# Attention and a Hyena gate on one core: gate tiles evicted by pairs of banks, spectra evicted by pairs, three table fetches, and a new order

## The chip, the cores and the metric

The kernel runs on one core of one Trainium2 chip. The metric is the device time of one execution in microseconds (us), lower is better, as the median of several executions. All matrix products are done in float16 or bfloat16 with float32 sums in PSUM; inputs and output are float32.

## The reference

Four batches of eight attention heads over 768 positions with 64 values each; every query sees the 96 positions up to its own and the first 8, with a distance bias whose slope depends on the head. The result, as 768 x 512 for each batch, goes through a Hyena gate: one projection into three parts, a circular convolution of the middle part along the sequence, a product of all three, and an output projection.

```
# q, k, v: (4, 8, 768, 64)
scores = q @ k^T / 8 - slope[h] * dist           # kept: own 96 positions, first 8
a = softmax(scores);  x = (a @ v) as (4, 768, 512)

proj = x @ w_proj                                # (512, 1536)
x1, x2, x3 = proj[..., :512], proj[..., 512:1024], proj[..., 1024:]
X2 = rfft(x2, axis=1);  H = rfft(filter_fft, axis=0)
y = x1 * irfft(X2 * H) * x3
out = y @ w_out                                  # (4, 768, 512)
```

## The kernel before

The kernel builds a graph of steps first and emits it afterwards. Each step (`Plan.op`) names the engines that may run it, what it reads and writes, and which PSUM banks it fills (`acq`) or empties (`use`). There are eight banks of 2 KB for each partition; they are cut from four tiles of two banks (`self.wide`), so banks 0 and 1, 2 and 3, 4 and 5, 6 and 7 are neighbours, and `Bank.two()` is a view over both of such a pair.

The order is written out by hand in the string `ORDER`. Each word is the number of a step, the letter of its engine (P TensorE, A ScalarE, V VectorE, G GpSimd, S SyncE) and the banks that it fills: `223P0` is step 223 on TensorE into bank 0. `schedule()` reads the words and `emit()` writes the instructions in that order. An engine runs its own instructions strictly in the order of the string and waits, by semaphores, for what the next one needs. A word such as `i1b4` is a matmul on zeros into bank 4 whose result nobody reads ("busy matmul", `busy`, L313). The string has 13 of them. DMA transfers are issued by the same queues: loads of inputs from GpSimd (POOL in the profile, L333), a few loads, the transposing transfers of batch 3 and all stores from SyncE (SP).

The work on one batch, in the names that the profile shows:

- **Loads.** q, k and v come as float32 and land as float16 in `qn`, `kn`, `vn`. In batch 0, q and k come in blocks of two heads (`load_pair`). Three of the four blocks go through GpSimd, the fourth through SyncE into `ot` as float32, and is cast.
- **Transposes.** TensorE turns q and k into `QT` and `KT` (L743 the pairs of batch 0, L786 the others). ScalarE or VectorE copies them out of their bank (L317, the helper `copy`). Batch 3 uses transposing DMA transfers instead.
- **Scores and exponentials.** For each pair of heads and each of three groups of key blocks, `scores` fills two neighbouring banks (L812). ScalarE takes the exponential of both in one instruction of 864 columns into `E` (L824), twelve for each batch. In batch 0, TensorE adds the distance bias in the bank beforehand (L598 to L605); in the others VectorE multiplies by a mask (L836).
- **Values.** `values` multiplies `E` by `vn`, with a column of ones for the sum (L862 and L867). VectorE takes the reciprocal, and VectorE or ScalarE scales the result into `xn` (L886, L891). TensorE transposes it (L914) into `xT`.
- **Gate.** For each of the four column blocks j of x1 and x3 and each half s of the sequence, `gate` computes two tiles of 128 x 384 (360 or 408 in batch 3): four matmuls each (L977, or L979 and L982 in batch 3), every tile into a bank of its own. The x1 tile is scaled into one of four staging buffers `x1` (helper `times`, L321 on ScalarE). The x3 tile is copied into `gt` by ScalarE (L991), and VectorE multiplies the two in place; or VectorE multiplies straight from the bank. There are 32 such pairs of tiles.
- **Convolution.** `butterfly` and `folded` fold `xT` on VectorE. The middle projection is done on the folded rows (L1050) and evicted to `ab`. `spectra` transforms it in three pairs of slots (L706): one matmul of 512 columns into a bank for each slot, each bank evicted to `X` by an instruction of its own (L317). VectorE multiplies by the filter's spectrum (`h1`, `h2`). The spectrum of the filter itself is computed once, early (`spectrum`, L715 on TensorE, its sums on VectorE). `inverses` turns back into `eo` (L1137 to L1142), `mixed` and `gated` combine the halves and multiply by `gt` into `y` (L1192 to L1197).
- **Output.** Six output tiles for each batch (L1101), evicted to `ot` (L321) and stored by SyncE. The last one is done in two halves of 256 columns.

The order interleaves these: while batch b is convolved, the attention of batch b + 1 runs between. Ahead of it all stand setup steps: the tables of sines for the transforms (`tables`: angles by TensorE, reduced by ScalarE and VectorE, L462 the copy on ScalarE, L476 the sine), the distance masks on GpSimd, and one small activation on ScalarE, a sine on two values, ahead of anything else there.

The lines that set how a pair of spectra is evicted (`PAIR_X` is empty in this kernel, so the second form is used for all twelve pairs):

```python
if (b, n) in self.PAIR_X:
    bks = [g.bank(), g.bank()]
    self.transform(b, pair, bks)
    g.op("AV", self.evac(1024), lambda e: self.copy(
        e, X[:, pair[0]:pair[0] + 2], bks[0].two()), use=bks, ...)
for s in () if (b, n) in self.PAIR_X else pair:
    bk = g.bank()
    self.transform(b, (s,), [bk])
    g.op("AV", self.evac(512), lambda e, s=s, bk=bk: self.copy(e, X[:, s], bk.f32()), ...)
```

Of the kernel before, what the change touches and what calls it, by code (L numbers as in the profile page):

```python
# [41 lines left out]
0V 32G 19S 4V 5V 34V 28S i1b0 i1b1 16S 8G 33V i1b2 15V 209A i1b3 3G 210A 54V 9V 206A i1b4 13V 204A 59A i1b5 22G 208A  # L42
1V 56V 6V 207A i1b6 57V 205A 25G 11V i1b7 21A 10V i1b0 24G 211A 223P0 53V 216V 35G 84P23 23G i1b1 51V 20V i1b4 2A 27G
213V 224A i1b5 18A 233P1 55V 58V 225V 218P4 26G 17V 234A 64P5 235V 219A 50G 52V 104P6 226V 65A 220V 38G 105V 76P0
106P5 77A 42G 221V 29V 78P6 222A 39G 107V 66A 227A 79A 41G 62P0 60V 239V 228P5 63A 80V 36G 212V 43G 85P 30V 90P4 37V
236V i1b7 215V 44G 81P01 61V 108V 91V 87P67 86A 40G 88P 240V 14V 92P4 229A 89A 73P23 31S 93V 82P 74P 67P67 75A 214V
12V 68P 83A 241V 70P23 230V 217V 231V 71P 69A 112P01 113P 72A 246V 109P45 272G 110P 94A 114A 115P23 247V 273G 101P67
111A 95P01 248V 274G 96P 102P 249V 116P 97A 98P45 280G 250V 99P 117A 118P01 282G 251V 103A 123P23 100A 119V 270G 124V
158P67 252V 125V 253P4 271G 120V 133P23 255P5 281G 159V 134V 160V 258P0 256A 260P1 279G 254A 135V 163P67 261A 257V 46G
259A 266P23 164V 128P45 165V 47G 268A 136P0 267A 372P1 48G 129V 130V 370P6 373A 166P7 285G 121P2 167V 131P3 263P45  # L50
371A 7V 132V 287G 368P1 137V 265A 126P3 374V 369V 161P0 122A 288G 397P5 127A 162V 382P67 264A 398V 377P23 45G 380P01
383A 395P4 189V 286G 399V 144P5 378A 396V 169P6 49G 195V 146A 188V 381A 402P23 499G 375P45 196V 174P7 403A 197V 275G
153P0 190V 176A 198V 148P1 171A 191V 496G 376A 155V 440P6 154P7 199V 284G 441A 150V 405P45 192V 156A 407P23 289G
400P01 200V 406A 193V 183P6 157V 379V 408A 290G 139P7 442P4 401A 194V 444P5 201V 500G 138P2 443V 445A 143P3 141A 384V
446A 185A 449P45 454P01 140A 145V 293P6 450A 278G 262V 404V 455A 452P23 283G 276S 447P45 149P7 409V 453A 277S 497G
242P0 202V 151A 305P1 448A 498G 203V 173P7 306A 147V 514G 152V 297P4 142V 456V 291G 295P1 237A 298A 512G 309P5 269V
175A 451V 294A 511G 390P23 243A 319P4 597P6 310A 391V 506G 392V 307P7 320A 598V 244A 507G 296A 317P4 410P23 308V 232A
393P1 599A 508G 318A 411V 299P6 177V 179P7 412V 394A 415P45 245A 321V 513G 300A 669P0 385P23 416V 181A 417V 593P1 505G
670A 595P7 386V 322V 594A 462P45 724G 387V 313P6 596A 301P0 463V 311P1 509G 457P23 302A 464V 314A 388P0 517G 238V 312A
607P45 458V 303V 184P6 723G 459V 413P1 178P7 292G 389V 608A 622P2 304V 168P0 501G 186A 315V 180A 418P3 620P6 623V 504G  # L60
414A 667P7 170A 726S 621V 419A 605P45 515G 602P01 187V 727S 606A 665P6 182V 420P3 624V 733G 172V 603A 668V 460P2 426P4
666V 510G 461A 422V 630P67 428A 632P01 609V 735G 625P23 631A 465P5 421P4 466V 722G 626A 671V 425P6 487V 633A 627P23
721G 488V 478P5 502S 427A 628A 473P0 503S 316V 737G 431P1 480A 490V 423A 738G 489V 600P23 475A 674P67 672P45 433A 634V
430P0 601A 739G 435P1 491V 673A 734G 325P2 424V 329P3 437A 629V 335P4 675A 736G 331P1 530P5 326V 332A 516G 492V 432A
333P2 676V 330A 725G 679P01 334A 677P67 337P3 336A 604V 323P2 680A 732G 518P4 493V 324A 640P01 338A 434V 494V 531A
327P2 731G 483P3 678A 641V 495V 468P5 743G 328A 642V 519A 610P67 339V 740G 635P01 485A 470A 611V 544P4 340V 534P3 612A
728G 636V 341V 520P5 637V 742G 681V 826S 615P01 535A 741G 682P67 521A 616V 342V 545A 467P3 744G 823S 683V 617A 343V
522P2 429V 344V 822S 477P4 523A 345V 472P5 684V 825S 613P2 474A 436P0 469A 348V 538P5 438A 526P6 524P3 614A 643P7 729S
439V 542P0 479A 638P1 346V 532P2 525A 824S 539A 349V 618P3 482P4 533A 850S 543A 476V 362P5 347V 484A 619A 536P0 546V
848S 685P4 537A 687P23 639V 363A 541V 359P1 686A 481V 527A 688V 486V 353P0 689V 644A 891S 360A 834P67 540V 832P45 354A  # L70
827P23 690P1 847S 528V 835A 650P0 691V 828A 529V 829P67 364S 660P1 713V 833A 849S 655P2 652A 547V 661P3 662A 712V 894S
830A 350P0 663A 715V 365P1 657A 892S 664V 351A 714V 851P23 366A 858P67 853P45 471V 893S 859A 552P0 716V 356P1 831V
553A 854A 550P6 730S 558P0 717V 548P7 357A 836V 355S 554P4 852A 367S 656P5 718V 361S 549A 560P1 842P23 658A 719V 556P7
551A 562P5 843V 561A 855V 645P6 559A 557A 646P1 720V 563A 555A 651P7 844V 648A 659V 647A 900P45 845S 856P01 564V 901A
837P23 565V 698P6 857A 838V 352S 707P4 566V 839V 653A 693P5 700A 649V 841S 709A 567V 902P23 897P67 695A 895P01 654V
898A 697P4 568V 846S 860V 702P5 896A 861P67 903A 569V 840S 708P0 862V 570V 692P1 863A 904V 747P2 899V 703P3 694A 710A
910P67 865S 573V 705A 699A 866P01 748A 911V 760P4 701V 864S 704A 867V 912V 868A 762P5 696V 914S 711V 758P6 574V 763A
905P01 571V 761A 870S 766P7 759A 764P4 906V 745P5 767A 572V 869S 765A 749P7 706V 746A 769V 773P6 913S 907V 771P5 774A
751P4 578P2 772A 768V 908S 750A 871P3 775V 752A 753P7 770V 584P6 754A 909S 776V 876P4 585A 755V 779P5 873A 358S 756V
791P7 878A 581P6 792A 757V 780A 783P3 936V 787P7 777P5 788A 887P4 784A 935V 781P7 789P0 872P3 790A 782A 938V 785P1  # L80
575P0 786A 937V 778A 877P1 889A 939V 874A 886P7 793V 940A 587P3 794V 888A 941V 957P4 795A 890V 942V 944P7 958A 796V
588A 590P5 943V 945A 589S 879A 972P3 797V 586S 970P7 591A 959P4 875V 973A 798V 971A 961P5 799V 960A 948P7 974V 962A
800V 579A 963P1 965P5 964A 946P4 580S 802V 966A 592S 882P1 947A 967V 916P5 949A 968V 582A 950P4 952P7 975V 951A 931P2
583S 969V 953A 921P4 884A 955V 576A 997P3 930P1 954V 933A 577S 998A 978P0 880V 982P2 956V 932A 993P3 983A 881P7 803V
994A 980P1 883A 995P2 991P3 801V 996A 976P6 926P7 992A 885V 977A 1000V 925P3 979A 999V 981A 934V 920P6 1001V 927A 985V
928A 915P1 984V 1002V 986A 819P7 929V 917A 1003V 987V 816P3 1004V 820A 988V 918A 1005V 821S 813P2 923A 989V 919V 922A
810P4 990V 817A 1021V 814A 818S 804P5 924V 811A 1019V 815S 1022V 807P2 812S 805A 1020V 1029P3 808A 1006V 1023P5 1008V
# [113 lines left out]

class Fused:
    PERIOD = 40.0
    PAIR_X = ()
    PAIR_AB = ()
    PAIR_EO = ()
    PAIR_T = (1, 2, 3)
# [1175 lines left out]
```

## Time and profile before

| | |
|---|---|
| median of 3 runs | 168.0 us (167.95 to 168.52) |
| the profiled execution, its own time | 167.31 us |
| its span, first to last instruction | 165.6 us |
| granted TensorE clock, mean over the span | 0.977 of full speed |
| moved by DMA | 22.84 MB, mean 138 GB/s |

The profile is one execution. PE is the matmul side of TensorE and PEld its weight loads, which overlap the matmuls; DVE is VectorE, ACT is ScalarE, POOL is GpSimd, SP is SyncE. A line such as L824 is a line of the kernel. "E<-bank" is the output and the input by the program's names. The form behind it (128x864 f16<-128x864 f32) is partitions x elements and type, and x48 the number of instructions. In a timeline the first column is the start in us from the start of the span and the second the length; consecutive instructions of one form are one row, and square brackets give the idle time ahead of it with what ended it. "PE bank" as the waiting side means that TensorE was about to write into a bank; the name behind the arrow is the engine, the tile and the line that released it. The page also cuts the span in 40 slices of 4.1 us; a digit there is a share in tenths. Ends of matmuls are modelled.

### The profile page before, as it was taken

How to read it: one execution, taken by the hardware profiler on the slowest of the kernel's cores; microseconds unless marked ns; L12 is line 12 of the kernel's file. 1: busy time of each engine (PE TensorE's matmuls, PEld its weight loads, DVE VectorE, ACT ScalarE, POOL GpSimd, SP SyncE). 2: the span in 40 equal slices, each digit the busy share in tenths (PEclk: the TensorE clock that was granted, in tenths of full speed). 3: DMA queues.
4: the chain of work that ended last, by engine and by line, in shares of the span. 5: the costliest groups of instructions: out<-in, count | busy, mean ns of one | idle time of the engine just before them, and what ended most of it. 6: DMA issues, size and time to landing. Idle time of an engine off the chain costs nothing.

```text
span 165.6 us, 4471 instructions
## 1 busy us (share of the span) xinstructions
PE 156.5 (95%) x1722; PEld 98.6 (60%) x1722; DVE 151.4 (91%) x351; ACT 149.9 (91%) x308; POOL 73.5 (44%) x94
## 2 busy tenths in 40 slices
PE   6758999999999999999999999999999999999990
PEld 2255756785654787657766655866655754585440
DVE  6698598999998999999999999999999999999940
ACT  3979697799999999999998999999997899999842
POOL 7997489999299996999930000000000000000000
PEclk9985899999999999999999999999999999999999
DMA  5999999999999999999999754603123203430685
GB/s 140 167 173 200 151 161 139 153 170 190 164 156 147 148 143 154 162 164 146 146 110 185 110 127 95 209 16 98 33 60 80 72 0 129 149 110 0 242 314 204
DMA packets 90365, 22.84 MB, mean 138 GB/s; under 512 B 81504, under 2 KB 87016, under 8 KB 90344
## 3 DMA queue, kind: packets, MB, share of 16 engines
q0 software_dynamic: 74880, 12.46, 100.8%
q1 hardware_dynamic: 15464, 10.10, 22.4%
q8 instruction: 13, 0.21, 0.5%
q14 instruction: 8, 0.07, 0.1%
HBM read 25.69 MB, written 6.29 MB: 193 GB/s over the span
## 4 chain that ended last, share of the span: by engine, by line
PE 87%; ACT 7%; DVE 3%; issue 1%; POOL 1%; ACTq 0%; POOLq 0%
PE bank L977 19%; PE bank L1050 13%; PE bank L1101 12%; PE bank L812 7%; PE bank L979 6%; PE bank L862 4%; PE bank L786 4%; PE bank L867 3%; PE bank L706 3%; PE bank L914 3%; ACT E L824 2%; PE bank L598 2%; ACT mask L613 1%; PE bank L604 1%; PE bank L1137 1%; PE bank L1140 1%
## 5 line engine op out<-in xcount | busy, mean ns | idle before, releaser
L824 ACT ACTIVATE E<-bank 128x864 f16<-128x864 f32 x48 | 41.9, 947 | 1.9 <-PE bank L812 1.9
L977 PE MATMUL bank<-xT,w 128*128 128x384 f16 x192 | 36.0, 326 | 0.0
L333 POOL DMA_DIRECT2D vn<-in_v_dram x28 | 25.9, 937 | 3.1 <-DMA w<-in_moe_w_proj_dram 2.9
L977 PEld LDWEIGHTS <-w 128*128 128x128 f16 x192 | 17.3, 98 | 10.7 <-issue 1.1
L1101 PE MATMUL bank<-wo,y 128*128 128x512 f16 (+1 forms) x100 | 22.7, 370 | 0.0
L333 POOL DMA_DIRECT2D kn<-in_k_dram x24 | 21.6, 908 | 0.5 <-issue 0.3
L333 POOL DMA_DIRECT2D qn<-in_q_dram x21 | 18.6, 887 | 6.2 <-PE bank L812 3.4
L836 DVE TENSOR_TENSOR E<-E,mask 128x1728 f16<-128x1728 f16 x18 | 18.6, 1048 | 0.0
L321 ACT ACTIVATE ot<-bank 128x512 f32<-128x512 f32 (+1 forms) x24 | 13.8, 605 | 3.2 <-PE bank L1101 3.1
L991 ACT CAST g<-bank 128x384 f16<-128x384 f32 (+2 forms) x32 | 15.9, 545 | 0.0
L862 PE MATMUL bank<-vn,E 128*128 128x65 f16 x224 | 15.4, 193 | 0.4 <-ACT E L824 0.4
L886 DVE TENSOR_TENSOR xn<-bank,rc 128x512 f16<-128x512 f32 (+1 forms) x20 | 15.6, 789 | 0.2
L1050 PE MATMUL bank<-w,xab 128*128 128x512 f16 x64 | 15.4, 379 | 0.0
L862 PEld LDWEIGHTS <-E 128*128 128x128 f16 x224 | 14.1, 97 | 2.2 <-issue 0.4
L1101 PEld LDWEIGHTS <-y 128*128 128x128 f16 x100 | 9.4, 98 | 9.9 <-DVE y L1197 0.5
L867 PE MATMUL bank<-vn,E 128*128 128x65 f16 x192 | 15.2, 193 | 0.0
L321 ACT ACTIVATE x<-bank 128x384 f16<-128x384 f32 (+2 forms) x28 | 14.4, 537 | 0.5 <-ACT ab L317 0.5
L317 ACT CAST X<-bank 128x512 f16<-128x512 f32 x24 | 13.8, 619 | 0.6 <-PE bank L706 0.5
L317 ACT CAST eo<-bank 128x384 f16<-128x384 f32 x31 | 13.5, 520 | 0.7 <-PE bank L1142 0.7
L867 PEld LDWEIGHTS <-E 128*128 128x128 f16 x192 | 13.2, 97 | 1.5 <-issue 0.6
L317 ACT CAST ab<-bank 128x512 f16<-128x512 f32 x23 | 13.9, 641 | 0.1
L812 PE MATMUL bank<-QT,KT 64*128 64x216 f16 (+2 forms) x224 | 13.6, 244 | 0.2 <-DVE KT L317 0.2
(186 smaller groups left out, 368.4 us busy)
## 6 DMA issues: line engine op xcount, KB each, us to landing
out_dram<-ot SPq DMA_DIRECT2D x23, 256.0 KB, 2.2
vn<-in_v_dram POOLq DMA_DIRECT2D x28, 120.0 KB, 7.7
kn<-in_k_dram POOLq DMA_DIRECT2D x21, 120.0 KB, 6.3
qn<-in_q_dram POOLq DMA_DIRECT2D x18, 128.0 KB, 5.8
w<-in_moe_w_proj_dram POOLq DMA_DIRECT2D x4, 256.0 KB, 6.7
g<-in_moe_filter_fft_dram POOLq DMA_DIRECT2D x1, 768.0 KB, 10.4
kn<-in_k_dram POOLq DMA_DIRECT2D x3, 192.0 KB, 6.4
qn<-in_q_dram POOLq DMA_DIRECT2D x3, 192.0 KB, 6.1
```

Of the source, the lines that this page charges most:

```text
L317: {"A": nc.scalar.copy, "V": nc.vector.tensor_copy, "G": nc.gpsimd.tensor_copy}[e](out, in_)
L321: self.nc.scalar.mul(out, in_, c)
L333: return self.g.op(eng, 0.57 + 0.00035 * nbytes[0] if eng == "G" else 0.5, lambda _: e.dma_start(dst, src), w=w, r=r, nbytes=nbytes, name= ...
L812: nc.tensor.matmul(bs[hh].f32()[:, off:off + w], self.KT[hs, hp, P * m:P * m + P], self.QT[hs, hp, KL * m:KL * m + w], start=(off == 0 and ...
L824: g.op("A", act(864), lambda _: nc.scalar.activation(eo, bs[0].two()[:, :, 0:432].rearrange("p h (m w) -> p h m w", m=2), Act.Exp, scale=s ...
L836: g.op("V", dve(1728, 2), lambda _: nc.vector.tensor_mul(ep, ep, mk), r=[("mask", h) for h in range(hs.start, hs.stop)] + ([("mask0", hp - ...
L862: nc.tensor.matmul(o[:, n, hh], ef[:, at:at + P], vt[:, t, 2 * hp + hh, 0:D + 1], start=first, stop=(t == 0), skip_group_check=True)
L867: nc.tensor.matmul(o[:, n, hh], ef[:, at:at + P], vt[:, t - 1, 2 * hp + hh, 0:D + 1], start=False, stop=True, skip_group_check=True)
L977: nc.tensor.matmul(bk.f32()[:, 0:h], w, self.xT[:, c, lo:lo + h], **kw)
L991: first = g.op("AV", {"A": act(h), "V": 0.0005}, lambda e: nc.scalar.copy(x3, pts[1].f32()[:, 0:h]) if e == "A" else None, use=[pts[1]], w ...
L1050: nc.tensor.matmul(bk.f32(), src[:, c], w[:, c, DM:2 * DM], start=(c == 0), stop=(c == 3))
L1101: nc.tensor.matmul(bk.f32()[:, 0:n], y[:, c, P * t:P * t + P], self.wo[:, c, ns], start=(c == 0), stop=(c == 3))
```

## The change

The change has four parts.

**Gate.** One step now does the eight matmuls of both tiles, the x1 tile into the first and the x3 tile into the second of two neighbouring banks (the loop over the four matmuls of a tile is now the function `gated_tile`). One instruction of 2 x 384 columns, on ScalarE or VectorE, scales both banks into a buffer `x13`, each by the root of the factor that x1 alone was scaled by. There are two such buffers (`XS`) in place of four for x1. VectorE multiplies the two halves of the buffer into `gt`.

**Spectra.** `PAIR_X` holds all twelve pairs, so both transforms of a pair fill two neighbouring banks and one instruction of 1024 columns evicts them.

**Activations in the setup.** In place of one sine on two values there are three activations on two values each: a sine, an exponential and an exponential ("fetch"). The order puts one exponential at the very start of ScalarE's queue, the other after the last exponential of the attention, and the sine at the end of the program.

**Order.** The string is a new one. It has 26 busy matmuls in place of 13 (23 of them ahead of the first values matmuls, in place of 13). In the built program ScalarE has 268 instructions in place of 310, VectorE 347 in place of 353; 31 of the wide gate evictions are on ScalarE and one on VectorE. Two copies of `QT` in batch 0 move from ScalarE to VectorE. Of batch 0's six pair loads on GpSimd the first is the same, the others follow in another order. The score matmuls behind the first values group stand in 22 runs in place of 16.

```diff
 ORDER = """
...
-0V 32G 19S 4V 5V 34V 28S i1b0 i1b1 16S 8G 33V i1b2 15V 209A i1b3 3G 210A 54V 9V 206A i1b4 13V 204A 59A i1b5 22G 208A
...
-1014A 1033A 1015S 1034S
+0V 34G 18S 9V 6V 30S 7V i1b0 11V i1b1 21S 10G 35V i1b2 14V i1b3 5G 60V 17V i1b4 54V i1b5 24G 36V 197A i1b6 58V 190A 8V
...
+947A 923V 948S 940P7 921V 938A 939S 927P0 941A 945S 930P1 942S 928A 929S 924P7 931A 932S 925A 926S 2A
 """
...
 class Fused:
     PERIOD = 40.0
-    PAIR_X = ()
+    PAIR_X = {(b, n) for b in range(4) for n in range(3)}
     PAIR_AB = ()
+    XS = 2
...
-        self.x1p = t("x1", [P, 4, 408])
-        self.x1 = [self.x1p[:, i] for i in range(4)]
+        self.x13 = t("x13", [P, self.XS, 2, 408])
...
-        self.warm = t("warm", [1, 2], F32)
+        self.warm = t("warm", [1, 8], F32)
...
-        g.op("A", 0.2, lambda _: nc.scalar.activation(self.warm, self.warm, Act.Sin),
-             r=["warm"], w=["warm"], table="sin", bias=-4000)
+        for i, (fn, table) in enumerate(((Act.Sin, "sin"), (Act.Exp, "exp"), (Act.Exp, "exp"))):
+            g.op("A", 0.11, lambda _, i=i, fn=fn: nc.scalar.activation(
+                self.warm[:, 2 + 2 * i:4 + 2 * i], self.warm[:, 0:2], fn), r=["warm"], w=[("warm", i)],
+                table=table, name="fetch", bias=-4000)
...
-        pts = []
-        for o in (0, 2 * self.DM):
-            bk = g.bank()
-
-            def run(_, o=o, bk=bk):
-                for c in range(4):
...
-            g.op("P", pe(*([360, 48] if cross and s else [h]) * 4), run, acq=[bk], r=xs + [("w", o // P + j)], name="gate")
-            pts.append(bk)
-        x1, key = self.x1p[:, self.turn4 % 4, 0:h], ("x1", self.turn4 % 4)
+        bks = [g.bank(), g.bank()]
+
+        def both(_):
+            for o, bk in ((0, bks[0]), (2 * self.DM, bks[1])):
+                self.gated_tile(o, bk, j, s, lo, h, cross)
+        g.op("P", pe(*([360, 48] if cross and s else [h]) * 8), both, acq=bks,
+             r=xs + [("w", j), ("w", 2 * self.DM // P + j)], name="gate")
+        n = self.turn4 % self.XS
         self.turn4 += 1
-        g.op("AV", self.evac(h), lambda e: self.times(e, x1, pts[0].f32()[:, 0:h], X1_SCALE),
-             use=[pts[0]], w=[key], name="x1")
-        x3, ko = gt[:, j, lo:lo + h], ("g", b % 2, j, s)
-        first = g.op("AV", {"A": act(h), "V": 0.0005}, lambda e: nc.scalar.copy(
-            x3, pts[1].f32()[:, 0:h]) if e == "A" else None, use=[pts[1]], w=[ko], name="x3")
-        then = g.op("V", dve(h, 2), lambda _: nc.vector.tensor_mul(
-            x3, x3 if then.alt == "A" else pts[1].f32()[:, 0:h], x1), use=[pts[1]], r=[key], w=[ko], name="g")
-        first.then, then.svc = then, dve(h, 1, True)
+        xx = self.x13[:, n, :, 0:h]
+        g.op("AV", self.evac(2 * h), lambda e: self.times(e, xx, bks[0].two()[:, :, 0:h], X1_SCALE ** 0.5),
+             use=bks, w=[("x1", n)], name="x13")
+        g.op("V", dve(h, 2), lambda _: nc.vector.tensor_mul(gt[:, j, lo:lo + h], xx[:, 0], xx[:, 1]),
+             r=[("x1", n)], w=[("g", b % 2, j, s)], name="g")
+
+    def gated_tile(self, o, bk, j, s, lo, h, cross):
+        nc = self.nc
+        for c in range(4):
+            w, kw = self.w[:, c, o + P * j:o + P * j + P], dict(start=(c == 0), stop=(c == 3))
+            if not cross:
+                nc.tensor.matmul(bk.f32()[:, 0:h], w, self.xT[:, c, lo:lo + h], **kw)
+                continue
+            nc.tensor.matmul(bk.f32()[:, 0:360].rearrange("p (t r) -> p t r", t=3), w,
+                             self.xTt[:, c, 3 * s:3 * s + 3, 0:KL], skip_group_check=True, **kw)
+            if s:
+                nc.tensor.matmul(bk.f32()[:, 360:408], w, self.xTt[:, c, 6, 0:48], start=False,
+                                 stop=(c == 3), skip_group_check=True)
```

The output is also evicted differently at the end: the last tile to be evicted and stored is a whole one of 512 columns, where it was a half of 256.

97 lines of the change are left out of this document (42 added, 55 removed).

## The prediction

> **What bounds the kernel now.** I read the page first (shares, slices, clock, chain), then TensorE's waits, then stretches of the timeline, then windows.
>
> ```profile
> PE 156.5 (95%) x1722; PEld 98.6 (60%) x1722; DVE 151.4 (91%) x351; ACT 149.9 (91%) x308; POOL 73.5 (44%) x94
> PE   6758999999999999999999999999999999999990
> PEclk9985899999999999999999999999999999999999
> PE 87%; ACT 7%; DVE 3%; issue 1%; POOL 1%; ACTq 0%; POOLq 0%
> ```
>
> TensorE is busy 95% of the span and carries 87% of the chain; VectorE and ScalarE are nearly as full. Does TensorE ever wait for them? Its waits, the whole answer (who <- whom: total, times, longest):
>
> ```profile
> PE bank L743 <- DMA kn<-in_k_dram: 1.8, 1, 1.8
> PE bank L313 <- DVE eo L399: 1.3, 1, 1.3
> PE bank L743 <- DVE QT L317: 0.6, 1, 0.6
> PE bank L505 <- DVE KT L317: 0.4, 1, 0.4
> PE bank L862 <- ACT E L824: 0.4, 2, 0.3
> PE bank L743 <- DVE y L468: 0.3, 1, 0.3
> PE bank L598 <- DVE eo L580: 0.2, 1, 0.2
> PE bank L812 <- DVE KT L317: 0.2, 1, 0.2
> ```
>
> All of these producers belong to the start. The last wait in time is that for the exponentials (L862), at the first values matmuls:
>
> ```profile
> 26.18 0.24 PE L862 MATMUL bank<-vn,E 128*128 128x65 f16 x2
> ...
> 27.66 0.19 PE L862 MATMUL bank<-vn,E 128*128 128x65 f16 x1 [0.26 <-ACT E L824]
> ...
> 28.44 0.38 PE L715 MATMUL bank<-pp,fwd 128*128 128x512 f16 x1
> ...
> 151.17 10.71 PE L1101 MATMUL bank<-wo,y 128*128 128x512 f16 x52
> ```
>
> So from 27.66 us to the end of the last matmul (151.17 + 10.71 = 161.9) TensorE waits for nobody. The kernel has two parts: a start that ends when the twelve exponentials of batch 0 are done, and 134 us in which TensorE's own work is the time. Faster evictions can't shorten the second part; only the start and the few us behind the last matmul can shrink. What sets the start is ScalarE:
>
> ```profile
> 15.01 1.28 ACT L824 ACT_TABLE_LOAD   x1
> 16.30 0.89 ACT L824 ACTIVATE E<-bank 128x864 f16<-128x864 f32 x1
> 17.09 0.38 ACT L462 ACTIVATE y<-bank 128x256 f32<-128x256 f32 x1
> 18.49 0.89 ACT L824 ACTIVATE E<-bank 128x864 f16<-128x864 f32 x1 [1.03 <-PE bank L812]
> 19.97 3.24 ACT L824 ACTIVATE E<-bank 128x864 f16<-128x864 f32 x4 [0.58 <-PE bank L812]
> ...
> 25.15 3.24 ACT L824 ACTIVATE E<-bank 128x864 f16<-128x864 f32 x4 [0.25 <-PE bank L812]
> ```
>
> The last of the twelve ends at 25.15 + 3.24 = 28.39, and 1.03 + 0.58 + 0.25 = 1.86 us of that is waiting for scores. They come late because TensorE has half its clock there (columns: length; PE, PEld, DVE, ACT, POOL busy; granted clock; DMA share; GB/s):
>
> ```profile
> 7.78:11.19 3.41, 1.71 (x64) 1.66 (x65) 3.28 (x12) 3.16 (x9) 3.41 (x5) 1.00 1.13 162
> 11.19:14.61 3.42, 2.17 (x40) 1.71 (x39) 3.27 (x10) 2.72 (x7) 3.42 (x6) 0.50 1.20 194
> 14.61:18.02 3.41, 3.41 (x33) 2.19 (x33) 2.44 (x12) 2.83 (x4) 0.81 (x1) 0.50 1.79 178
> ```
>
> **Wider evictions.** All 32 gate tiles lose two evictions of some 384 columns and gain one of 768; the 24 X evictions become 12 of 1024.
>
> ```profile
> 148.07 2.01 ACT L317 CAST eo<-bank 128x384 f16<-128x384 f32 x5
> 143.78 1.07 ACT L317 CAST X<-bank 128x512 f16<-128x512 f32 x2
> ```
>
> Queued without gaps, five 384-wide casts take 2.01, two 512-wide ones 1.07, four 864-wide exponentials 3.24 (above). So each adds 0.40, 0.53 and 0.81 at most: about 0.09 us for each 100 columns and 0.07 of fixed cost, which makes an estimated 0.72 for 768 and 0.93 for 1024. A gate tile saves 0.08 of ScalarE, an X pair 0.13, in all 32 x 0.08 + 12 x 0.13 = 4 of 150 us, and four small evictions that VectorE did come back to ScalarE. None of it lies on the path: I value it at nothing. What hides it is TensorE's unbroken work; without that cover it would be worth up to 4.
>
> What it adds is a wait. The eviction now waits for both tiles, so the first bank stands full for the second tile's four matmuls, and with two staging buffers in place of four it also waits for the product of two tiles back. Queued behind it on ScalarE are exponentials and other evictions, and TensorE waits for their banks. No such wait is in the trace; I take 0 and keep 2.3 as the other end (below). VectorE keeps one product for each gate tile, sheds four evictions, gains one wide one and a few copies: within 0.5 us, nothing on the path.
>
> **Start.** The first key load stays the first on POOL, so TensorE's 1.8 us wait for it stays. The other five pair loads stand behind it in another order and the loads of values, weights and batch 1 behind those; POOL has them all on their way before TensorE's need (no wait for a load past the start now), and I cost their order at 0. On ScalarE, ahead of the first exponential, two query copies and a small key copy go (to VectorE), and a small cast, an angle copy (0.38, as at 17.09) and a sine come. Table loads ahead of it stay three.
>
> ```profile
> 12.41 0.63 ACT L476 ACTIVATE fwd<-y 128x512 f16<-128x512 f32 x1 [0.70 <-DVE y L468]
> ...
> 13.08 0.41 ACT L476 ACTIVATE fwd<-y 128x256 f16<-128x256 f32 x1
> 13.40 0.90 ACT L317 COPY KT<-bank 128x720 f16<-128x720 f16 x2
> 14.18 0.81 ACT L317 COPY QT<-bank 128x768 f16<-128x768 f16 x1
> ```
>
> -2 x 0.81 + 0.41 + 2 x 0.38, with the small copies about even, is -0.5: first exponential at about 15.8 in place of 16.30. Behind it come the same twelve, with a pair of key copies (0.90) in place of the angle copy: 28.39 - 16.30 = 12.1, less 1.86, less 0.38, plus 0.90, is 10.8. End at 26.6 with no score late, a gain of 1.8.
>
> Whether scores are late hangs on the clock. The built order has 23 busy matmuls (L313) ahead of the first values in place of 13; ten of them stand behind the first key transposes, where now the clock falls. But 1.71 us of work lost it and 2.17 did not regain it; the new order, idle till the key load at about 9.2 and dense behind it, has some 2.0 in the window 7.78:11.19. I take it that this window still loses the clock, and that the next one, now dense, regains it at 14.61 in place of 18.02. Half speed for 3.4 us delays 1.7 us of TensorE's work, of which I let 0.3 reach ScalarE, whose queue is loaded till 15.8: gain 1.5. Bounds: 0 (both windows lost again) and 2.5 (no score late and the 0.70 wait at 12.41 gone too). By the Trainium skill (TensorE: Matmul & The Clock Gate, Part 1) one busy window of about 3.4 us releases the clock and one idle window takes it. The trace agrees on the length and on the fall; that 2.17 of 3.42 us did not count as busy is only in these rows.
>
> Behind the exponentials the spectrum matmuls (L715) follow the last values group directly. Now they start at 28.44 without waiting for VectorE's sums; TensorE would be there 1.5 earlier, the sums perhaps not: +0.3 (0 to 0.6).
>
> The three table fetches: one finds its table loaded, one only moves a load of 1.28 ahead, and the sine's, last in the program, adds a load of 1.28 behind the last eviction, beside the last store: 0.
>
> **More work for TensorE.** The built order has 22 separate runs of score matmuls behind the first values, where now there are 16 (the same 168 matmuls). A run costs something at both ends:
>
> ```profile
> 37.40 1.46 PE L977 MATMUL bank<-xT,w 128*128 128x384 f16 x8
> 38.80 0.55 PE L812 MATMUL bank<-QT,KT 64*128 64x216 f16 x8
> 39.28 2.12 PE L977 MATMUL bank<-xT,w 128*128 128x384 f16 x12
> 41.24 0.39 PE L786 MATMUL bank<-ident,qn 128*128 128x128 f16 x4
> ```
>
> Twelve gate matmuls take 41.24 - 39.28 = 1.96, 0.163 each; the eight ahead of the scores take 1.40 in place of 1.30, 0.10 more. Eight score matmuls of 216 columns, two at a time on half the rows each, would take 0.37 at this rate and take 0.48, 0.11 more. A run costs 0.21, six cost 1.3, with no cover since TensorE is the bound there; 0 if each fell into a wait. The Trainium skill (TensorEngine Tiling (Array Packing), Key Properties) says that a change of tiling mode drains TensorE. It gives no figure; the trace agrees with its 0.21.
>
> Two more busy matmuls stand past the values groups:
>
> ```profile
> 5.86 0.81 PE L313 MATMUL bank<-eo 128*128 128x512 f16 x3
> ```
>
> At 0.21 (512 columns at the rate above) they add 0.4.
>
> **End.**
>
> ```profile
> L321 ACT ACTIVATE ot<-bank 128x512 f32<-128x512 f32 x10 | 5.8, 612 | 2.8 <-PE bank L1101 2.8
> L321 ACT ACTIVATE ot<-bank 128x256 f32<-128x256 f32 x2 | 0.8, 380 | 0.0
> 155.40 1.02 DVE L1197 TENSOR_TENSOR y<-y,g 128x768 f16<-128x768 f16 x2
> ```
>
> The last eviction and store move half a tile; in the new order a whole one: 0.612 - 0.380 = 0.23, and a little for the transfer. VectorE's products for the last six output tiles are done at 156.4, and TensorE is there at 151.17 + 5.2 = 156.4 too, so a delay counts there; a wide gate eviction now stands ahead of the last casts: 0.1. Together +0.35 (0 to 0.8).
>
> **Sum.** -1.5 + 0.3 + 1.3 + 0.4 + 0.35 = +0.85 on the profiled execution of 167.31 (span 165.6): 168.2. That execution is 0.7 under the median of 168.0, so 168.9. A change within 0.5% (167.2 to 168.8) can't be told from none.
>
> **Rivals.**
> - *Full clock throughout*: gain 1.8, 168.6. For it, ten busy matmuls at the right place; against, 2.17 was not enough.
> - *Faster: ScalarE's start contracts.* Gain 2.5, no wait for the sums, no longer end: -2.5 + 1.7 = -0.8, 167.2, and 166.9 if half of the new score runs also fall in front of a wait. It decides if the last batch-0 exponential ends before 26. For it: ScalarE sheds only work; against: all four query copies now queue on VectorE.
> - *Slower: pairs of banks are waited for.* One gate tile in four makes TensorE wait the 0.72 - 0.40 = 0.32 by which its eviction is longer: 8 x 0.32 = 2.5, 171.4. It decides if TensorE's waits name the gate or exponential past 30 us. For it, both evicting engines are 91% busy in strict order; against, not one such wait now.
> - *Nothing moved*: 168.0.
>
> **Chances.** Forecast 0.36 (168.3 to 169.5, about half on each side of the bound: slower 0.19, no change 0.17); full clock 0.16 (no change 0.12, faster 0.04); contracted start 0.24, faster; bank waits 0.20, slower; nothing moved 0.04. Faster 0.28, no change 0.33, slower 0.39. The range runs from under the contracted start, 166.6, to the bank waits, 171.4.
>
> **What would show it.** Right: the last batch-0 exponential near 26.9; clock 0.5 in one window in place of two; no TensorE wait past 30 us; gaps of 0.2 around 22 runs of scores; ScalarE some us less busy to no effect. Wrong: a last matmul that ends before 161, or bank waits in the middle.

## The result, and the profile after

The changed kernel takes 168.84 us (median of 18 executions, 167.57 to 170.99), the kernel before 167.81 (median of 18, 167.17 to 168.52). The ratio is 1.0064, 95% interval 1.0038 to 1.0090: slower by 0.6%. The forecast was 168.9. The slowest of the 18, 170.99 at a mean clock of 0.978, is left out of the ratio and of the counts below. The profiled execution of after took 169.06, with a span of 167.4.

The page of after, the lines that answer to those of before:

```profile
PE 159.7 (95%) x1735; PEld 97.7 (58%) x1735; DVE 152.7 (91%) x345; ACT 151.5 (91%) x266; POOL 73.2 (44%) x94
PE   6989998999999999999899899999999999999990
PEclk9999999999999999999999999999999999999999
PE 66%; ACT 17%; DVE 7%; DMA 5%; issue 2%; ACTq 1%; SPq 0%; DVEq 0%
```

TensorE is still busy 95% of the span, but its share of the chain fell from 87% to 66%: ScalarE, VectorE and a transfer now stand in the chain, in the middle of the program. The clock is full throughout. TensorE's waits, the whole answer:

```profile
PE bank L309 <- DVE eo L395: 1.3, 1, 1.3
PE bank L309 <- DVE y L466: 0.7, 1, 0.7
PE bank L309 <- ACT E L822: 0.5, 2, 0.3
PE bank L810 <- DMA KT<-kn: 0.4, 1, 0.4
PE bank L810 <- DVE xn L884: 0.2, 1, 0.2
PE bank L309 <- ACT xn L888: 0.2, 1, 0.2
PE bank L704 <- DVE xT L313: 0.2, 1, 0.2
```

Four of these seven name L309, a busy matmul: work that nobody needs, waiting in TensorE's queue for a bank. Three are in the middle, where before had none. TensorE's timeline shows where they lie:

```profile
8.05 0.53 PE L741 MATMUL bank<-ident,kn 96*64 96x96 f16 x16
...
25.94 0.38 PE L309 MATMUL bank<-eo 128*128 128x512 f16 x1 [0.26 <-ACT E L822]
...
28.36 0.38 PE L309 MATMUL bank<-eo 128*128 128x512 f16 x1 [0.22 <-ACT xn L888]
28.57 0.38 PE L713 MATMUL bank<-pp,fwd 128*128 128x512 f16 x1
...
82.46 0.60 PE L704 MATMUL bank<-ab,fwd 128*128 128x512 f16 x2 [0.21 <-DVE xT L313]
83.30 0.36 PE L810 MATMUL bank<-QT,KT 64*128 64x216 f16 x6 [0.23 <-DVE xn L884]
...
95.34 0.36 PE L810 MATMUL bank<-QT,KT 64*128 64x216 f16 x4 [0.45 <-DMA KT<-kn]
```

The brackets give the engine's idle time. From the start of one matmul to the start of the next, less the first one's own length, TensorE loses 0.4 at each of the two rows near 82 and 83, and 0.6 at 95.

ScalarE's timeline at the start, and at the end:

```profile
14.37 1.28 ACT L611 ACT_TABLE_LOAD   x1
...
15.96 1.65 ACT L822 ACTIVATE E<-bank 128x864 f16<-128x864 f32 x2
...
19.50 7.17 ACT L822 ACTIVATE E<-bank 128x864 f16<-128x864 f32 x9
26.54 1.76 ACT L888 ACTIVATE xn<-bank,rc 128x64 f16<-128x64 f32 x8
...
163.42 0.60 ACT L317 ACTIVATE ot<-bank 128x512 f32<-128x512 f32 x1 [0.22 <-PE bank L1099]
164.03 1.28 ACT L398 ACT_TABLE_LOAD   x1
165.33 0.20 ACT L398 ACTIVATE warm<-warm 1x2 f32<-1x2 f32 x1
```

The last exponential of batch 0 ends at 19.50 + 7.17 = 26.67, 1.72 earlier than before. But the first spectrum matmul (L713) starts at 28.57 where before's started at 28.44: the gain is not there any more two microseconds later.

To compare two orders, TensorE's work can be counted. Each matmul counts as long as its columns take at full clock (0.213 us for 512, at least 0.027); score matmuls and pair transposes, which run two at a time, count half, and busy matmuls nothing. That makes 137.27 us in both kernels. The times at which each profiled execution had done so much of it:

| work done | before | after | after - before | between the row above and this one |
|---|---|---|---|---|
| 5 | 18.45 | 16.40 | -2.05 | transposes and first scores |
| 14 | 30.43 | 29.86 | -0.57 | the end of the start, two busy matmuls |
| 22 | 39.61 | 38.33 | -1.28 | spectra, transposes in another order |
| 60 | 81.45 | 80.95 | -0.50 | score runs, a busy matmul |
| 62.5 | 84.09 | 84.69 | +0.60 | the waits for xT and xn |
| 72 | 93.75 | 94.39 | +0.64 | |
| 75 | 97.00 | 98.56 | +1.57 | the wait for KT |
| 137.27 | 161.81 | 163.22 | +1.40 | batch 3, nothing changes |

Behind the last matmul the end of the span follows after 3.8 us before and 4.15 after, +0.36. So the new order was ahead for 81 us, lost its lead in two places in the middle, and some more at the end.

These two executions differ by 1.75 us, the medians by 1.03: the profiled one of after is the slowest of its 12 at full clock, that of before one of its faster ones. Both kernels have levels. After ran 12 times with a clock of 0.998 or more (median 168.50; "at full clock" below means 0.994 or more) and 5 times with 0.984 to 0.990 (median 169.86, 1.36 more). Before, in 23 executions that ran beside the last experiments, had 14 at a clock of 0.976 to 0.979 (median 167.76) and 9 at 0.969 (168.54).

### The profile page after: what moved, and what is told of

The parts are those of the page before. It is cut to its first block, busy times and chain, and to the rows that moved or that the text cites. A ratio compares the mean times of both kernels' runs of the same rounds, so it can differ in the third digit from the quotient of the medians.

```text
span 167.4 us, 4455 instructions
## 1 busy us (share of the span) xinstructions
PE 159.7 (95%) x1735; PEld 97.7 (58%) x1735; DVE 152.7 (91%) x345; ACT 151.5 (91%) x266; POOL 73.2 (44%) x94
## 4 chain that ended last, share of the span: by engine, by line
PE 66%; ACT 17%; DVE 7%; DMA 5%; issue 2%; ACTq 1%; SPq 0%; DVEq 0%
PE bank L987 14%; PE bank L1099 13%; PE bank L1048 10%; ACT E L822 6%; PE bank L989 6%; PE bank L810 4%; PE bank L784 4%; DMA KT<-kn 3%; PE bank L860 2%; PE bank L704 2%; DMA X<-in_v_dram 2%; PE bank L865 2%; ACT xn L888 2%; PE bank L912 2%; ACT x L317 1%
## 5 line engine op out<-in xcount | busy, mean ns | idle before, releaser
L822 ACT ACTIVATE E<-bank 128x864 f16<-128x864 f32 x48 | 41.0, 904 | 0.7 <-PE bank L810 0.6
L987 PE MATMUL bank<-xT,w 128*128 128x384 f16 x192 | 35.0, 326 | 0.0
L317 ACT ACTIVATE x<-bank 128x768 f16<-128x768 f32 (+2 forms) x31 | 24.9, 817 | 3.3 <-DVE g L979 2.3
L884 DVE TENSOR_TENSOR xn<-bank,rc 128x512 f16<-128x512 f32 (+1 forms) x21 | 16.5, 787 | 0.4
L317 ACT ACTIVATE ot<-bank 128x512 f32<-128x512 f32 (+1 forms) x25 | 14.4, 592 | 2.5 <-PE bank L1099 2.5
L810 PE MATMUL bank<-QT,KT 64*128 64x216 f16 (+2 forms) x224 | 14.5, 242 | 0.7 <-DMA KT<-kn 0.4
L313 ACT CAST ab<-bank 128x512 f16<-128x512 f32 x22 | 12.9, 600 | 1.8 <-PE bank L1048 1.8
L313 ACT CAST eo<-bank 128x384 f16<-128x384 f32 x30 | 12.8, 534 | 0.0
L810 PEld LDWEIGHTS <-KT 64*128 64x128 f16 x224 | 7.8, 94 | 8.7 <-issue 6.0
L309 PE MATMUL bank<-eo 128*128 128x512 f16 x26 | 10.1, 491 | 2.7 <-DVE eo L395 1.3
```

The costliest lines, as they stand in the source:

```text
L313: {"A": nc.scalar.copy, "V": nc.vector.tensor_copy, "G": nc.gpsimd.tensor_copy}[e](out, in_)
L317: self.nc.scalar.mul(out, in_, c)
L810: nc.tensor.matmul(bs[hh].f32()[:, off:off + w], self.KT[hs, hp, P * m:P * m + P], self.QT[hs, hp, KL * m:KL * m + w], start=(off == 0 and ...
L822: g.op("A", act(864), lambda _: nc.scalar.activation(eo, bs[0].two()[:, :, 0:432].rearrange("p h (m w) -> p h m w", m=2), Act.Exp, scale=s ...
L884: nc.vector.tensor_mul(to, o[:, :, :, 0:D], rc.to_broadcast([P, 2, 2 * nt, D]))
L987: nc.tensor.matmul(bk.f32()[:, 0:h], w, self.xT[:, c, lo:lo + h], **kw)
```

## The experiments

Each kernel is timed in several rounds beside the kernel before on the same chip; ratios are to that one. In a diff, "-" is the changed kernel, or the version named, and "+" the experiment.

**1. Narrow evictions in the new order.** Gate tiles and spectra as before, with `gate` of before and each step of the order split into its two halves at its place; all else as after.

```diff
-    PAIR_X = {(b, n) for b in range(4) for n in range(3)}
+    PAIR_X = ()
...
-        self.x13 = t("x13", [P, self.XS, 2, 408])
+        self.x1p = t("x1", [P, 4, 408])
```

> The changed kernel with its order, but every gate tile and every spectrum evicted by itself again: four matmuls, then four, each bank with its own 384-wide eviction, four x1 buffers and the product in place; twelve more X evictions of 512. Only the two forms of eviction are undone; start, busy matmuls, loads and the runs of scores stay. Theory (the wider evictions are worth nothing, TensorE's work is the time behind the start): 168.8, within 0.5 us of the changed kernel's 168.84, with ScalarE some 4 us busier. Rival 1 (the wide evictions hold pairs of banks and make the queues late, which is the wait at 82 us): faster, 168.0, and that wait is gone. Rival 2 (in this order ScalarE's 4 us do lie on the path between 64 and 84 us): slower, 170 or more, with TensorE waiting for ScalarE there.

Measured: 170.08 (6 executions), ratio 1.0104 (1.0062 to 1.0147). Four of the six had lost a window of the clock, with a median of 170.12 where after has 169.86 at that level; the two with full clock took 168.11 and 169.30. At the same clock the difference is about 0.2, and the rest is how often the clock fell. ScalarE is busy for 154.2 us in place of 151.5, 2.7 more. TensorE waits for ScalarE once past 30 us, 0.3 at 40, and not between 64 and 84, so the median over 170 is not what the second rival describes; the first one's 168.0 is not reached either. Experiment 4 repeats this with the clock held.

**2. Without the three late busy matmuls.**

```diff
-125P23 237V i1b6 120P45
+125P23 237V 120P45
...
-238V i1b2 267G
+238V 267G
...
-416P4 i1b5 412P5
+416P4 412P5
```

> The changed kernel without the three busy matmuls that stand behind the first values group (two around the end of the start, one in the middle of batch 1's gates). Theory (0.21 us each where TensorE is the bound, the first two partly in front of waits): 0.2 to 0.6 us faster, 168.4. Rival (they keep the clock up or fill waits that are there anyway): no change, or a granted clock below 1 and slower.

Measured: 167.72 (12 executions), ratio 0.9985 (0.9953 to 1.0017). That is 1.1 under after, more than expected, and 167.22 against 168.50 at full clock. Its profile shows why three matmuls of 0.21 cost 1.3. VectorE around the first values groups, in after:

```profile
26.79 0.21 DVE L889 RECIPROCAL rc<-bank 128x8 f32<-128x8 f32 x1 [0.79 <-PE bank L865]
27.03 0.69 DVE L884 TENSOR_TENSOR xn<-bank,rc 128x512 f16<-128x512 f32 x1
27.64 0.59 DVE L679 TENSOR_SCALAR g<-g 128x512 f16<-128x512 f16 x1
28.15 0.28 DVE L680 TENSOR_SCALAR g<-g 128x512 f16<-128x512 f16 x1
```

The same in this experiment, and its first spectrum matmul:

```profile
26.04 0.21 DVE L889 RECIPROCAL rc<-bank 128x8 f32<-128x8 f32 x1 [0.15 <-PE bank L865]
26.28 0.69 DVE L884 TENSOR_TENSOR xn<-bank,rc 128x512 f16<-128x512 f32 x1
26.89 0.28 DVE L679 TENSOR_SCALAR g<-g 128x512 f16<-128x512 f16 x1
27.09 0.29 DVE L680 TENSOR_SCALAR g<-g 128x512 f16<-128x512 f16 x1
```

```profile
27.35 0.38 PE L713 MATMUL bank<-pp,fwd 128*128 128x512 f16 x1
```

In after a busy matmul stands between the two first values groups and waits for a bank that an exponential still reads (the row at 25.94). The values group behind it comes 0.7 later, and VectorE's reciprocal waits for it (0.79). The filter's last sums stand behind that reciprocal in VectorE's queue and end at 28.43 in place of 27.38. The spectrum needs the sums and starts 1.22 later. 0.11 of this comes from ahead of it: the last exponential ends at 26.67 in after and at 26.56 here. From that end to the first spectrum matmul, the profiles of all five versions of the new order that have these three matmuls take 1.9 us, those of all eight without them 0.8. So the three cost 1.1 at this place.

**3. The clock.** First three more busy matmuls, placed in a wait of TensorE.

```diff
-56V 64P1 207V i1b2
+56V 64P1 i1b6 i1b7 i1b5 207V i1b2
```

> The changed kernel with three more busy matmuls behind the fourth pair transpose, in the 0.72 us in which TensorE waits for VectorE at 10.4 us. So far, executions whose stretch from 7.8 to 11.2 us had 2.40 us or more of TensorE work kept the clock, and those with 2.22, 1.71 lost it. Theory (the spread of the changed kernel, 167.6 to 169.9, is this: in 12 of its 17 undisturbed runs the clock is 0.995 or more, with a median of 168.5, in five it is 0.984 to 0.990, with 169.86): clock 1.0 in every run, median 168.5, none above 169.3. Rival (the matmuls come on top, 0.2 us each): 169.1. Rival (the clock falls for another reason): the two levels stay.

Measured: 168.32, ratio 1.0021 (1.0001 to 1.0041). All twelve executions have a clock of 0.995 or more, and none is over 169.01. The upper level of after is the clock. The later experiments bear it out: in all 70 executions of the seven versions with these three matmuls the clock is 0.994 or more, while after and the three versions with its 23 and without the three lost it in 18 of 48.

Then ten fewer, those between the key transposes and the first values group (six of them shown).

```diff
-211V i1b5 52G 39V i1b6 67A 212V i1b7 206V
+211V 52G 39V 67A 212V 206V
...
-207V i1b2 59V 219P5 65V 41G i1b3 108P2
+207V 59V 219P5 65V 41G 108P2
...
-70P i1b0 47G
+70P 47G
```

> The changed kernel without the ten busy matmuls between the first key transposes and the first values group, so with 13 at the start as before. Theory (these ten hold the clock, and a lost window costs 1.4): clock 0.96 to 0.98 in every run, two windows at half, last exponential of batch 0 near 29, median 170 to 170.5. Rival (the start is early because of ScalarE's and the loads' order, and the busy matmuls only cost time): 168.0 to 168.5.

Measured: 168.45, ratio 1.0021 (0.9995 to 1.0047), clock 0.975 to 0.986. The clock falls, as expected, and the time doesn't rise. The theory that these ten are worth 1.4 fell; the rival is right. ScalarE's row:

```profile
18.47 7.19 ACT L822 ACTIVATE E<-bank 128x864 f16<-128x864 f32 x9
```

This is the fastest of the twelve, at 167.32, with one window at half clock; ten of the others have a lower clock, 0.975 to 0.980. In it the last exponential ends at 25.66, a microsecond earlier than after's, although 3.4 us ran at half clock. Ten busy matmuls are 10 x 0.213 = 2.1 us of TensorE's queue in the part of the start where ScalarE waits for it; that they take as much as the clock gives fits the numbers. The windows of this kernel and of experiment 1, set to where the clock changes (columns as in the prediction):

```profile
7.36:10.78 3.42, 1.82 (x50) 1.47 (x51) 2.61 (x8) 3.40 (x8) 3.42 (x5) 1.00 1.16 173
10.78:14.19 3.41, 3.21 (x50) 2.91 (x51) 3.31 (x11) 3.28 (x8) 3.41 (x5) 0.50 1.15 172
14.19:17.60 3.41, 3.41 (x75) 2.26 (x75) 3.38 (x10) 3.40 (x7) 1.14 (x2) 1.00 1.40 185
```

```profile
9.08:12.49 3.41, 2.22 (x56) 1.34 (x51) 3.30 (x12) 2.53 (x5) 3.41 (x4) 1.00 1.00 140
12.49:15.91 3.42, 3.42 (x37) 2.30 (x31) 2.56 (x6) 3.40 (x6) 2.86 (x4) 0.50 1.22 199
```

The stretch at half clock is 3.4 us long here and there, and twice that in before (6.8), but starts at 10.78 here, at 12.49 there and at 11.19 in before: the windows lie differently in these three executions, of three kernels. (The 2.40 in the expectation was counted between fixed times, not in these windows, and bounds nothing.) So one kernel could keep or lose the clock by where its wait of 0.7 us near 10.5 falls, which would make the two levels of after. That is not shown: there is no profile of after on its upper level, and executions differ in the start itself (TensorE waits 0.47 at 9.3 in the profile of experiment 1, and not in after's). By the Trainium skill (TensorE: Matmul & The Clock Gate, What's actually happening) the window runs freely and doesn't start with the kernel; the three different starts agree.

**4. The SyncE queue, and a mended version.** In after the first scores of batch 3 wait for the transposed keys. First, the copy of the value rows is moved behind the transfers.

```diff
-675G 671S 324V
+675G 324V
...
-761S 441V
+761S 671S 441V
```

> The changed kernel with one step moved on SyncE's queue: the copy of the global value rows (which waits 11.8 us for a value load) stands behind the first five transposing transfers of batch 3 instead of ahead of them. Theory (these transfers start late because they stand behind that copy, and the scores wait for KT at 94.7 us): they start before 84.7, the 0.45 us wait of TensorE for KT near 95 is gone, 0.6 us faster: 168.2. Rival (they could not start sooner anyway, because the loads of batch 3 or the scores of batch 2 end then): 168.8.

Measured: 168.26, ratio 1.0027 (0.9999 to 1.0055); at full clock 168.16 against 168.50. The first transfer is issued at 81.97 in place of 84.67, but the scores still start at 95.06, after 0.8 of waiting (put down to the eviction of xT there, which ends at the same moment). So the time is the theory's and its mechanism is not: the wait it wanted to remove is still there, and 0.3 at full clock is small beside the scatter of either kernel there (1.3 and 1.5 from lowest to highest).

A version with this, with the clock held (3) and without late busy matmuls (2) was run with wide and with narrow evictions.

> The changed kernel with the three busy matmuls that hold the clock, without the three behind the first values group, and with SyncE's copy of the value rows behind the first transposing transfers. Theory (the parts add: 168.5 with full clock, 1.3 less for the late busy matmuls as their full-clock runs showed, 0.3 less for the transfers): 166.9, clock 1.0 in every run, faster than before (167.85) by about 0.5%. Rival (they overlap, since an earlier TensorE meets the other engines' queues): 167.5.

> The kernel with the three mends (clock held, no late busy matmuls, SyncE's copy later), but with gate tiles and spectra evicted by themselves. Theory (the wide evictions are worth nothing; the 1.2 us by which the first run of this kind was slower came from the clock, lost in 4 of 6 runs, and runs with full clock differ by 0.2): within 0.4 us of the mended kernel with wide evictions, about 167.0. Rival (with TensorE earlier, ScalarE's 4 us lie on the path): 168 or more, with waits of TensorE for ScalarE between 64 and 90 us.

Measured: wide 168.71 (ratio 1.0018, 0.9987 to 1.0048), narrow 168.64 (1.0031, 1.0011 to 1.0052), twelve executions each, all with full clock. The wide evictions are worth nothing that can be measured here; that theory holds, though not its 167.0. The rival's time of 168 or more is met without its reason: the narrow version's waits for ScalarE past 30 us come to 0.3, at 39. The sum of 166.9 fell, and the profile of the wide version shows on what. Its TensorE row, then the transfer in its chain, and the same of after:

```profile
95.38 0.36 PE L810 MATMUL bank<-QT,KT 64*128 64x216 f16 x4 [1.39 <-DMA KT<-kn]
```

```profile
87.40 7.93 DMA KT<-kn
```

```profile
90.04 5.25 DMA KT<-kn
```

Issued at 87.40 or at 90.04, the key tile lands at 95.3: the issue isn't what sets it. The wide version has two levels at full clock, 167.2 to 167.8 five times and 168.6 to 169.7 seven times. In the profiles, after and these three versions, which wait, issue the last load of batch 3 from POOL at 84.08 to 84.60; before, experiment 2 and both of 3, which don't, at 82.87 to 83.86. That the transposing transfers queue behind those loads fits; it was not tested. Experiment 1 issues the load later still, at 85.09, and doesn't wait, but its scores come at 96.72, 1.4 later than after's.

**5. Other work in front of those scores.** As the mended version, but with SyncE's queue as in after and two output tiles ahead of the first scores of batch 3.

```diff
-765P67 597A 342P2 819S 636V 602A 491V 333P3 766A
+597A 342P2 819S 636V 602A 491V 333P3 765P67 766A
```

> The changed kernel with the three busy matmuls that hold the clock, without the three late ones, and with the first score matmuls of batch 3 (which waited for the transposed keys near 94 us) moved behind two output tiles, 1.8 us of TensorE's work; SyncE's queue as in the changed kernel. Theory (what is left of the spread, two levels 1.5 us apart at full clock, is that wait for transfers that land near 95 us whenever they are issued): one level, 167.2, no wait for KT, 0.4% faster than before. Rival (the wait moves to the next scores, or the later exponentials hold up batch 3): 168.2, still two levels.

Measured: 168.61, ratio 1.0045 (1.0028 to 1.0062), five executions from 168.39 to 168.81. One level, but a new wait of the edit's own making: the next scores but one fill the same banks, and no output tile lies between any more.

```profile
96.77 0.55 PE L810 MATMUL bank<-QT,KT 64*128 64x216 f16 x8 [0.80 <-ACT E L822]
```

The same with 13 busy matmuls in all, none of them behind the first key transposes:

> The changed kernel with 13 busy matmuls, all at the start, as before: without the ten between the key transposes and the first values group and without the three behind it; the first scores of batch 3 behind two output tiles. Theory after the last runs (busy matmuls in a queue delay what stands behind them by about as much as the clock that they hold is worth): clock near 0.98, 167.9, within 0.7 us of the version that holds the clock. Rival (at full clock everything behind is earlier): 169 or more.

Measured: 168.65, ratio 1.0037 (1.0015 to 1.0058), clock 0.976 to 0.986. It misses the 167.9, but is level with its counterpart that holds the clock, with the same wait. That agrees with experiment 3: holding the clock with busy matmuls gains nothing here.

Then a third output tile between those scores and the next.

```diff
-333P3 765P67 766A 504V 784S 343A 500V 770P45 768P67 334A 763P01 505V 336P2
+333P3 343A 765P67 766A 336P2 334A 504V 784S 500V 770P45 768P67 763P01 505V
```

> As the version with the first scores of batch 3 behind two output tiles, clock held and no late busy matmuls, but with a third output tile between those scores and the next, since the next but one fills the same banks and waited 0.96 us for the exponential. Theory (that wait was the only cost of moving the scores, and the two levels are gone): 168.6 - 0.9 = 167.7, in one level. Rival (the exponentials of batch 3 are now late, and the wait turns up at its values): 168.4.

Measured: 168.06, ratio 0.9999 (0.9981 to 1.0018), twelve executions from 167.79 to 168.31. By the medians 0.55 of the 0.9 came back, by the ratios 0.8 (the kernel before took 167.83 beside the one and 168.10 beside the other), and the spread is the smallest of the kernels with twelve executions. Some 0.4 of waiting for an exponential is left. It equals the kernel before. No version beats that one beyond the measurement; experiment 2 comes nearest.

**6. More score runs.** On the version of 168.61, six runs of score matmuls cut in two, of which one is shown.

```diff
-362P45 355P67 141V 363A 414P2
+362P45 141V 363A 414P2 355P67
```

> The version with clock held, no late busy matmuls and later first scores of batch 3, with six runs of score matmuls cut in two: the second pair of banks stands behind the next TensorE step (a transpose, projection or inverse), so 27 runs where that version has 21. Nothing else changes. Theory (a run costs 0.15 to 0.21 us of TensorE's time): 0.9 to 1.3 us slower than that version. Rival (the switch is hidden in waits for banks and weights): within 0.3 us.

Measured: 170.54, ratio 1.0164 (1.0145 to 1.0183), 1.93 slower than its base, 0.32 for each cut. Between the two profiles, 2.2 us apart, gaps of TensorE over 0.15 us grow by 1.3 in sum, at score matmuls and transposes whose banks are freed later. The other 0.9 are left for the switches, about 0.15 each; the division is by that threshold, and not by a run.

**7. The wait at 82 us.** On the version of 168.06, one subtraction of the inverse transform goes behind the two evictions that TensorE waits for.

```diff
-323V 568P67 577V 487A 678G 583P45 569V 570V
+568P67 577V 487A 678G 583P45 569V 570V 323V
```

> The same, with one step moved on VectorE: a subtraction of the inverse transform (0.6 us, at 81.4 us in the changed kernel) stands behind the eviction of xT and the scaling of xn that TensorE waits for at 82 us, instead of ahead of them. Theory (TensorE loses 0.5 to 1.0 us there because VectorE's strict queue has this step first): 0.5 us faster than the version without this move, 167.2. Rival (VectorE is full there and what is put back is missed later, at the outputs): no change.

Measured: 168.70, ratio 1.0041 (1.0019 to 1.0064), slower by 0.6. TensorE's gaps at 82 stay at 0.28 and 0.21, and a new wait stands at 87:

```profile
PE bank L705 <- DVE xn L885: 0.4, 1, 0.4
```

The theory fell: what VectorE puts back is missed some five microseconds later. At the place that was freed VectorE has nothing to do, since the values aren't there yet:

```profile
81.13 0.21 DVE L890 RECIPROCAL rc<-bank 128x8 f32<-128x8 f32 x1 [0.56 <-PE bank L866]
```

So the subtraction had filled a wait of 0.56; what stands behind it comes later, and the xn that TensorE waits for at 87 starts at 86.05 in place of 85.23. What sets the gaps at 82 stays open.

## Why the prediction was right, point by point

The median came out as forecast, 168.84 against 168.9. The evictions and the end were right, the start right in size but not in its working, the busy matmuls mis-sized, and two waits were missing. The errors cancelled: that the median was met to 0.1 us is luck.

- *The start*, -1.5 forecast: the last exponential ends at 26.67 (forecast 26.9), a gain of 1.72. But "TensorE's 1.8 us wait for it stays" failed. The first key pair's transposes start at 8.05 in place of 9.19. Its load is issued at the same time (3.31 and 3.30) but landed at 7.48 in place of 9.14, and between 6.69 and 7.48 in all 13 profiles of the new order; the next pair load is issued at 4.88 in place of 4.08. So the 1.8 us wait for it is gone, and the order of the loads was costed at 0 without looking at the first of them; what brings it sooner was not tested. TensorE had 2.65 us of work between 7.78 and 11.19, where "some 2.0" was taken, and in 12 of 17 executions no window was lost. The rival *full clock* (0.16) was the common case; the forecast's one lost window happened in 5 of 17.
- *The sums*, +0.3, and *two more busy matmuls*, +0.4: these terms were mis-sized. The spectrum starts 1.9 after the last exponential, and with the late busy matmuls gone 0.8, without a wait of TensorE ahead of it (experiment 2). So the sums by themselves cost nothing, and the busy matmuls 1.1. The busy matmuls were priced at their own 0.21, as if only TensorE's time were at stake. Left out was that they wait for a bank in a strict queue and hold up the values that VectorE needs, whose results TensorE needs next.
- *Score runs*, +1.3: right in sign, somewhat high for the switches. Around score matmuls TensorE loses 2.3 us more in after than in before; 1.4 are the gaps at 82 and 95, and 0.9 are left for six runs, 0.15 each in place of 0.21. Where runs are cut and nothing else is rearranged, waits come on top, 0.32 (experiment 6).
- *Wider evictions, nothing*: right (experiments 1 and 4), and their prices too. On ScalarE:

```profile
57.17 2.84 ACT L313 CAST X<-bank 128x1024 f16<-128x1024 f32 x3
...
62.33 0.80 ACT L317 ACTIVATE x<-bank 128x768 f16<-128x768 f32 x1
63.03 0.53 ACT L313 COPY xT<-bank 128x480 f16<-128x480 f16 x1
```

  A gate eviction takes 0.70 in the queue (63.03 - 62.33) and an X eviction 0.95 (2.84 / 3), where 0.72 and 0.93 were estimated. "ScalarE some us less busy" failed: 151.5 against 149.9, since the new order gives it other work (one more table load of 1.28 and some casts); at the same order it saves 2.7, where 4 were estimated. The wait of a gate eviction for the product of two tiles back exists, 2.3 us in sum, and TensorE's waits don't name it:

```profile
ACT x L317 <- DVE g L979: 2.3, 3, 1.2
```

  With four buffers in place of two the kernel needs 210.8 KB of each partition, where 207.9 are there, so what this wait costs stays untested.

- *Bank waits*, taken at 0 of up to 2.3 (the rival itself has 2.5, and 8 x 0.32 is 2.6): none at the gates, but TensorE does wait past 30 us, at 82 for VectorE (0.8 in gaps, 1.1 by the table) and at 95 for KT (0.6 and 0.9). "No TensorE wait past 30 us" failed there, and bank waits in the middle were the forecast's own sign of being wrong. Their size belongs to this execution: in the profiles of experiments 2 and 3 the same steps lose 0.5 at 82 and nothing at 95. The first stands behind VectorE's strict queue, as that rival had it, but experiment 7 didn't shorten it by moving a step, so its cause is open; the second hangs on transfers of batch 3, which the forecast didn't follow: "POOL has them all on their way before TensorE's need" looked at the start only.
- *The end*, +0.35: +0.36. The sine's table load (164.03 to 165.3) lies beside the last store, as said.
- *The contracted start*, the rival at 0.24: the last exponential did not end before 26 in after, though it did in one version (25.66, experiment 3), which was no faster than before. Its 166.9 should be 166.6 (167.2 less half of 1.3), as the range has it.

The parts as measured: -1.7 for the start, +1.2 at its end (1.1 of it the busy matmuls), -0.7 for the spectra and transposes between 30 and 39 us (by the table, and in no step of the forecast), +0.9 for the score runs, +0.8 at 82, +0.6 at 95, +0.36 at the end: 1.5, where the two profiles differ by 1.76. The forecast's +0.85 from the same execution of before was lower. The medians differ by only 1.03, since the profiled execution of before was one of its fast ones, and that of after the slowest of its 12 at full clock.

## What to carry to other kernels

A filler matmul can cost what stands behind it, and not its own length alone: place it only where its bank is long free and TensorE would wait anyway, and ask which engine waits for the next real result. When a new order is compared, put both traces on one scale of work done; a gain that is lost again shows as a step at its place. Follow every queue that a reordering touches to the end of the program, also the ones that moved nothing themselves: here TensorE's wait for the transfers of the last batch was up to 1.39 us, nearly as much as the whole start had gained.

## What the runs showed of the hardware

- The stretch at half clock started at 10.78, 11.19 and 12.49 in three profiled executions. In windows of 3.41 us, counted forward and back from there, 1.71, 1.82, 2.17 and 2.22 us of TensorE work were followed by half clock, 2.69 (experiment 3, from 0.54), 2.82 (before, from 4.37) and more by full clock. After kept the clock in 12 executions and lost it for a while in 5, at 1.36 us.
- A transposing transfer holds SyncE for 1.2 us and more, but the data that TensorE waited for landed 5.25 and 7.93 us after the issue, at 95.3 in both profiles.
- The same first load, issued at 3.30, landed 5.8 us later in before, where the load behind it was issued at 4.08, and 3.4 to 4.2 us later in 13 profiles in which that one was issued at 4.87 to 4.89.
